# A two-layer GELU block: the first x chunk turned as two 64-row halves, block by block, with layer 1 started on the first blocks

## The chip, the cores and the metric

One core of a Trainium2 chip. The metric is the device time of one execution in microseconds (us), the median of several runs. A difference of less than 2% is called "same"; ratios with a 95% interval resolve some 0.3%. Engines are named as in the profile: PE is TensorE's matmul side, PEld its weight loads, DVE is VectorE, ACT is ScalarE, SP issues DMAs. The span is the time from the first to the last instruction of a traced run; a transfer "lands" when its data has arrived; PSUM is the memory into which TensorE writes here.

## The reference, cut to what matters

```python
B, S, D, F = 1, 2048, 448, 1792            # bf16
def reference(x, w1, b1, w2, b2):
    h = gelu_tanh(einsum("bsd,df->bsf", x, w1) + b1)
    return einsum("bsf,fd->bsd", h, w2) + b2
```

448 is 3 x 128 + 64, so each layer-1 product has three full blocks of 128 input features (k = 0, 1, 2) and a remainder of 64 (k = 3).

## The kernel before: the parts that matter

Layer 1 needs x with features on the partitions. The first chunk of 512 rows is loaded plainly and turned on TensorE; later chunks are turned by DMA. All matmuls of both layers contract 64 rows at a time: part "a" takes one half of the partitions, part "b" the other, for two output tiles at once, so that two matmuls run side by side, one on rows 0 to 63 of the array and one on rows 64 to 127. The 64 remainder rows of w1 are loaded to partitions 64 to 127 only (`w1r`); VectorE copies what the other half needs to partitions 0 to 63.

```python
H = 64; HC = 256; KT = 3; NWARM = 7
W1CUTS = (0, 4, 8, 14)                      # w1 in three transfers, by output tile
unit = [psum_tensor([128, 2, 512], FP32) for i in range(4)]    # two banks each
# ...
def turn(t):                                # 128 rows of x, one full turn for each k
    for k in range(KT):
        tensor.transpose(stage(t)[:, k*P:(k+1)*P], xn[:, t, k*P:(k+1)*P], ident)   # after "x"
def evac(engine, t):                        # PSUM -> xT, 384 columns, for all k; vector and scalar in turn
    ...
def turn_all():
    # vector: xr <- the remainder columns of xn
    # for t in 0..3: turn(t); evac(t)
    # tensor: two turns of xr; then vector and scalar copy them to xT[:, 3] (2 copies each)
# ...
warm(NWARM)          # dummy matmuls of 512 columns until x lands
warm(1, HC)          # half dummy
turn_all()
warm(1, HC)          # half dummy
turn_b1()            # vector: four 32x32 transposes of b1, then a cast
for i in (0, 1):     # vector: w1r, partitions 64..127 -> 0..63, event ("w1rU", i)
    ...
for h in (0, HC):    # pairs 0 and 1 of layer 1, part a, half the columns at a time
    L[0].a(h, h + HC); L[1].a(h, h + HC)
L[0].b(); L[2].a(); L[1].b()
for j in range(3, NPAIR):
    L[j].a(); L[j - 1].b()
L[-1].b()
# ... layer 2 of the chunk; then chunks 1 to 3
```

The matmul of k = 3 in part b waits for `w1r` (one output tile) or for VectorE's copy of it, `w1rU` (the other). VectorE works through its list in the order of the program, so what stands last on that list is done last.

## Time and profile before

| | before |
|---|---|
| median of 6 runs | 94.24 us (93.99 to 94.44) |
| the traced run | 94.75 us, span 93.44 |
| PE busy | 97% of the span |
| first turn / first layer-1 matmul / first w1r matmul | 4.00 / 5.79 / 8.155 us |

The page of the profile, before: busy time by engine (us, share, number of instructions), and the chain of work that ended last.

```profile
span 93.4 us, 2060 instructions
...
PE 90.4 (97%) x932; PEld 46.5 (50%) x932; DVE 13.3 (14%) x33; ACT 38.5 (41%) x63; POOL 1.7 (2%) x8
...
## 4 chain that ended last, share of the span: by engine, by line
PE 97%; DVE 0%; issue 0%
PE u L216 91%; PE u L191 4%; PE u L338 1%; DVE out_sb L325 0%; PE u L359 0%
```

The chain is TensorE's own work from start to end, so the time is TensorE's dense stream plus what comes ahead of it. L216 is the helper that issues every layer-1 and layer-2 matmul.

The timeline of the head, before (start, duration, engine, line, operation, tiles; in brackets the idle time of the engine before it and what ended it):

```profile
4.00 1.44 PE L338 MATMUL u<-ident,xn 128*128 128x128 bf16 x12
...
4.51 0.36 DVE L345 COPY xT<-u 128x384 bf16<-128x384 bf16 x1 [0.40 <-PE u L338]
...
5.44 0.42 PE L191 MATMUL u<-const-bfloat16-1.0 128*128 128x256 bf16 x1
...
5.76 0.60 DVE L368 COPY xT<-u 64x256 bf16<-64x256 bf16 x2 [0.25 <-PE u L359]
...
5.79 2.52 PE L216 MATMUL u<-xT,w_sb 64*128 64x256 bf16 x30
...
6.39 0.90 DVE L180 STREAM_TRANSPOSE b1t<-b1n 32x32 bf16<-32x32 bf16 x4
7.42 0.17 DVE L182 CAST b_f<-b1t 128x14 f32<-128x14 bf16 x1
7.63 0.49 DVE L382 COPY w1r<-w1r 64x256 bf16<-64x256 bf16 x2
...
8.15 0.38 PE L216 MATMUL u<-xT,w1r 64*128 64x512 bf16 x2
```

Read it as two lists. TensorE: turns from 4.00, half dummy at 5.44, layer 1 from 5.79, first w1r matmuls at 8.15. VectorE: a chain with hardly a pause from 5.76 (remainder copies, bias transposes, cast) whose last link, the w1r copy, begins at 7.63; the record of the first of its two parts, the one that pair 0 needs, ends at 7.85. TensorE wanted it for the weight load at 7.94, so VectorE was 0.1 us early.

How fast TensorE runs can be read from counts. Two windows of 0.6 us, before, PE only (us, busy and count, granted clock, DMA share, GB/s):

```profile
core 0: us, PE busy (x), PEclk, DMA share, GB/s
...
5.85:6.45 0.60, 0.60 (x9) 1.00 0.84 260
6.75:7.35 0.60, 0.60 (x16) 1.00 0.95 248
```

Both are fully busy with matmuls of 256 columns, but the second has nearly twice as many: pairs start 214 ns apart up to 6.62 us and 109 ns apart after. The column of the granted clock shows 1.00 in both, so it does not show this.

### The profile page before, as it was taken

The page shows a single profiled execution, that of the slowest core. Times are in us where ns is not written, and L with a number is a line of the kernel's source. Part 1 is how long each engine was busy: PE and PEld are TensorE (multiplying, and loading weights), DVE is VectorE, ACT ScalarE, POOL GpSimd, SP SyncE. Part 2 cuts the span into 40 slices and gives each one's busy share as a digit, 9 for nine tenths or more (in the row PEclk, how much of TensorE's full clock was granted, in tenths as well). Part 3 has the DMA queues.
Part 4 walks back from the last instruction along what each step waited for, and adds up shares of the span by engine and source line. Part 5 has one row for each costly group of instructions (what it writes and reads, how often), then busy time and mean ns, then how long its engine had stood idle before and what let it go on. Part 6 is the DMA issues. An engine that isn't in the chain of part 4 may idle for free.

```text
span 93.4 us, 2060 instructions
## 1 busy us (share of the span) xinstructions
PE 90.4 (97%) x932; PEld 46.5 (50%) x932; DVE 13.3 (14%) x33; ACT 38.5 (41%) x63; POOL 1.7 (2%) x8
## 2 busy tenths in 40 slices
PE   6999999999999999999999999999999999999990
PEld 2475444455544444454554444445544444475890
DVE  0173001010334000000234000000234000000421
ACT  6073787900002887900002888900001878910001
POOL 6000000000000000000000000000000000000000
DMA  2999999554748000000033000000022000000022
GB/s 51 358 275 292 360 309 151 113 113 91 83 86 217 7 0 0 7 0 0 0 102 101 0 0 4 0 7 0 0 98 98 0 0 7 0 0 7 18 80 98
DMA packets 12344, 7.32 MB, mean 78 GB/s; under 512 B 6960, under 2 KB 12144, under 8 KB 12336
## 3 DMA queue, kind: packets, MB, share of 16 engines
q1 hardware_dynamic: 11904, 6.80, 31.1%
q10 hardware_dynamic: 400, 0.39, 1.2%
q8 instruction: 7, 0.11, 0.5%
q14 instruction: 1, 0.01, 0.0%
q0 software_dynamic: 32, 0.00, 0.0%
HBM read 3.79 MB, written 1.84 MB: 60 GB/s over the span
## 4 chain that ended last, share of the span: by engine, by line
PE 97%; DVE 0%; issue 0%
PE u L216 91%; PE u L191 4%; PE u L338 1%; DVE out_sb L325 0%; PE u L359 0%
## 5 line engine op out<-in xcount | busy, mean ns | idle before, releaser
L268 ACT ACTIVATE g<-u,b_f 128x512 bf16<-128x512 f32 x56 | 35.0, 685 | 40.3 <-PE u L216 40.3
L216 PE MATMUL u<-w_sb,g 64*128 64x448 bf16 (+1 forms) x504 | 43.2, 328 | 0.0
L216 PE MATMUL u<-xT,w_sb 64*128 64x512 bf16 (+1 forms) x348 | 41.2, 372 | 0.0
L216 PEld LDWEIGHTS u<-w_sb,g 64*128 64x128 bf16 x504 | 24.4, 94 | 18.6
L216 PEld LDWEIGHTS u<-xT,w_sb 64*128 64x128 bf16 x348 | 16.9, 95 | 19.6 <-issue 0.3
L311 DVE TENSOR_TENSOR out_sb<-u,b_bc 128x448 bf16<-128x448 f32 x14 | 8.1, 619 | 60.6 <-PE u L216 60.6
L216 PE MATMUL u<-xT,w1r 64*128 64x512 bf16 x56 | 10.6, 376 | 0.0
L191 PE MATMUL u<-const-bfloat16-1.0 128*128 128x512 bf16 (+1 forms) x9 | 3.8, 578 | 0.8 <-PEq L443 0.8
L216 PEld LDWEIGHTS u<-xT,w1r 64*128 64x128 bf16 x56 | 2.7, 94 | 3.3
L328 ACT CAST out_sb<-u 128x224 bf16<-128x224 f32 x1 | 0.3, 346 | 9.2 <-PE u L216 9.2
L191 PEld LDWEIGHTS u<-const-bfloat16-1.0 128*128 128x128 bf16 x9 | 1.2, 138 | 2.4 <-issue 2.4
L345 ACT COPY xT<-u 128x384 bf16<-128x384 bf16 x2 | 1.0, 479 | 2.8 <-PE u L338 2.8
L175 ACT ACT_TABLE_LOAD x1 | 1.3, 1283 | 0.7 <-PEq L443 0.7
L338 PEld LDWEIGHTS u<-ident,xn 128*128 128x128 bf16 x12 | 1.2, 140 | 0.5 <-issue 0.5
L338 PE MATMUL u<-ident,xn 128*128 128x128 bf16 x12 | 1.4, 307 | 0.0
L186 DVE COPY xT<-xT 64x512 bf16<-64x512 bf16 x3 | 0.9, 290 | 3.5 <-DMA xT<-in_x_dram 3.5
L406 DVE COPY b_z<-b_bc 1x448 bf16<-1x448 bf16 x1 | 0.3, 267 | 6.8 <-DMA b_bc<-in_b_dram 6.8
L319 DVE TENSOR_TENSOR out_sb<-u,b_bc 128x448 bf16<-128x448 f32 x1 | 0.6, 625 | 1.7 <-PE u L216 1.7
L180 DVE STREAM_TRANSPOSE b1t<-b1n 32x32 bf16<-32x32 bf16 x4 | 0.8, 202 | 0.1
L345 DVE COPY xT<-u 128x384 bf16<-128x384 bf16 x2 | 0.7, 357 | 0.7 <-PE u L338 0.7
L368 ACT COPY xT<-u 64x256 bf16<-64x256 bf16 x2 | 0.7, 368 | 0.0
L352 DVE COPY xr<-xn 128x256 bf16<-128x256 bf16 x1 | 0.2, 227 | 3.0 <-DMA xn<-in_x_dram 3.0
(18 smaller groups left out, 5.0 us busy)
## 6 DMA issues: line engine op xcount, KB each, us to landing
out_dram<-out_sb SPq DMA_DIRECT2D x16, 112.0 KB, 1.7
w_sb<-in_w_dram SPq DMA_DIRECT2D x2, 784.0 KB, 8.7
w_sb<-in_w_dram SPq DMA_DIRECT2D x1, 576.0 KB, 6.4
xn<-in_x_dram SPq DMA_DIRECT2D x1, 448.0 KB, 3.1
w_sb<-in_w_dram ACTq DMA_DIRECT2D x1, 384.0 KB, 4.2
w_sb<-in_w_dram SPq DMA_DIRECT2D x1, 384.0 KB, 4.1
xT<-in_x_dram SPq DMA_TRANSPOSE x12, 4.5
w1r<-in_w_dram SPq DMA_DIRECT2D x1, 160.0 KB, 4.0
```

What stands on the lines that cost most here:

```text
L175: pr.op("scalar", lambda e: e.activation(junk[:, :], one, ACT.Gelu_apprx_tanh), event="table")
L180: pr.op("vector", lambda e, q=q: e.transpose(b1t[32 * q:32 * q + 32, :], b1n[:, 32 * q:32 * q + 32]), after=["b1n"], event=("b1t", q))
L186: pr.op("vector", lambda e: e.tensor_copy(xT[0:H, KT, s0:s1], xT[H:P, KT, s0:s1]), after=after, event=event)
L191: pr.op("tensor", lambda e: e.matmul(unit[0][:, 0, 0:cols], lhsT=ones_w, rhs=ones_m[:, 0:cols], start=True, stop=True))
L216: o = pr.op("tensor", lambda e: e.matmul(unit[u][:, lo, cols], lhsT=lhsT, rhs=rhs, start=start, stop=stop, skip_group_check=skip), after=a ...
L268: pr.op("scalar", lambda e, lo=lo, ft=ft: e.activation(g[:, ft, c * SC:(c + 1) * SC], unit[u][:, lo, :], ACT.Gelu_apprx_tanh, bias=b1_f[:, ...
L311: pr.op("vector", lambda e, lo=lo, j=j: e.tensor_tensor(out=out_sb[:, j, :], in0=unit[u][:, lo, 0:D], in1=b2_bc[:, :], op=ALU.add), after= ...
L319: pr.op("vector", lambda e: e.tensor_tensor(out=out_sb[:, j, :].rearrange("p (two h) -> p two h", two=2), in0=unit[u][:, :, 0:DH], in1=b2_ ...
L328: pr.op("scalar", lambda e: e.copy(out_sb[:, j, DH:D], unit[u][:, 1, 0:DH]), after=[y[1]], event=("o", j, 1))
L338: pr.op("tensor", lambda e, k=k: e.transpose(stage(t)[:, k * P:(k + 1) * P], xn[:, t, k * P:(k + 1) * P], ident[:, :]), after=["ident", "x ...
L345: pr.op(engine, lambda e: e.copy(o, i) if engine == "scalar" else e.tensor_copy(o, i), after=[("xt", t)], event=("xT0", t))
L368: e.copy(o, i) if engine == "scalar" else e.tensor_copy(o, i),
```

## The change

The intent: turn x in pieces of 64 rows, two side by side on the two halves of the array, so that a turn streams 64 columns instead of 128; drain each 128 x 256 block as soon as it is turned; let layer 1 wait for the block it reads, not for whole tiles; fill TensorE's wait by starting pair 0 and put the last turns inside it; load w1's first tiles as 2 + 2 so that the first lands earlier; drop the half dummies, and with them the switch from 128-row to 64-row matmuls after the turns.

```diff
-        W1CUTS = (0, 4, 8, 14)
+        W1CUTS = (0, 2, 4, 8, 14)
...
         load_w1(0, "scalar")
+        load_w1(1, "scalar")
...
-                            after += ([("xT0", 2 * h), ("xT0", 2 * h + 1)] if k < KT else
+                            after += ([("xT0", h, k)] if k < KT else
...                                             (turn, evac, turn_all replaced by:)
+        def turn(o, i, event, after):           # two turns of 64 rows, on the two halves of the array
+            for half, rows in enumerate(HALVES):
+                pr.op("tensor", lambda e, half=half, rows=rows: e.transpose(o(half), i(rows), ident[rows, rows]), ...)
+        def turn_block(h, k, u, i, wait=()):    # 256 rows of x, block k: two such turns
+        def drain_blocks(engine, h, ks, u, wait=None):     # PSUM -> xT, 256 columns for each block
+        def turn_first():
...                                             (vector: xr copy)
+            for k, engine in enumerate(("vector", "scalar", "vector")):
+                turn_block(0, k, k, 0)
+                drain_blocks(engine, 0, (k,), k)
+            turn_block(1, 0, 3, 0)
+            turn_block(1, 1, 3, 1)
+            drain_blocks("scalar", 1, (0, 1), 3)
+        def turn_rest():
+            turn_block(1, 2, 2, 0, [("xT0", 0, 2)])
...                                             (two remainder turns of xr into the same banks)
+            drain_blocks("vector", 1, (2,), 2, ("xr", 1))
...                                             (remainder copies, as before, after that drain)
         warm(NWARM)
-        warm(1, HC)
-        turn_all()
-        warm(1, HC)
+        turn_first()
+        L = [Layer1(0, j) for j in range(NPAIR)]
+        L[0].a(0, HC)
+        turn_rest()
         turn_b1()
...                                             (w1r copies, unchanged)
-        for h in (0, HC):
-            L[0].a(h, h + HC)
-            L[1].a(h, h + HC)
+        L[1].a(0, HC)
+        L[0].a(HC, SC)
+        L[1].a(HC, SC)
         L[0].b()
+        L[1].b()
         L[2].a()
-        L[1].b()
```

More of the change, by code (lines that the diff above doesn't have):

```diff
@@ L155, in bass_standalone__dense_activation_gelu__prompt_kernel @@
         load_w1r(0)
-        load_w1(1)
+        load_w1(2)
         load_w1r(1)
-        load_w1(2)
+        load_w1(3)
         load_w2(0, 7)
@@ L330, in drain, with spot @@
                     store(j, [("o", j, 0), ("o", j, 1)])
-        def stage(t):
-            return unit[3 - t // 2][:, t % 2, 0:2 * P].bitcast(BF16)
-        def turn(t):
-            for k in range(KT):
-                pr.op("tensor", lambda e, k=k: e.transpose(
-                    stage(t)[:, k * P:(k + 1) * P], xn[:, t, k * P:(k + 1) * P], ident[:, :]),
-                    after=["ident", "x"], event=("xt", t) if k == KT - 1 else None)
-        def evac(engine, t):
-            o = xT[:, 0:KT, t * P:(t + 1) * P]
-            i = stage(t)[:, 0:D3].rearrange("p (k s) -> p k s", k=KT)
-            pr.op(engine, lambda e: e.copy(o, i) if engine == "scalar" else e.tensor_copy(o, i),
-                  after=[("xt", t)], event=("xT0", t))
-            busy[(3 - t // 2, t % 2)] = ("xT0", t)
-        def turn_all():
+        HALVES = (slice(0, H), slice(H, P))
+        def spot(u, i, rows=slice(0, P)):
+            return unit[u][rows, :, i * H:(i + 1) * H].bitcast(BF16).rearrange("p b (t s) -> p b t s", t=2)
+        def turn(o, i, event, after):
+            for half, rows in enumerate(HALVES):
+                pr.op("tensor", lambda e, half=half, rows=rows: e.transpose(o(half), i(rows), ident[rows, rows]),
+                      after=["ident"] + after, event=event if half else None)
+        def turn_block(h, k, u, i, wait=()):
+            for t in (0, 1):
+                turn(lambda half, t=t: spot(u, i)[:, half, t, :], lambda rows, t=t: xn[rows, 2 * h + t, k * P:(k + 1) * P],
+                     ("xt", h, k) if t else None, ["x"] + list(wait))
+        def drain_blocks(engine, h, ks, u, wait=None):
+            n = len(ks)
+            o = xT[:, ks[0]:ks[0] + n, h * HC:(h + 1) * HC].rearrange("p k (t b s) -> p k b t s", b=2, t=2)
+            f = unit[u][:, :, 0:n * H].bitcast(BF16).rearrange("p b (k t s) -> p k b t s", k=n, t=2)
+            for i in range(n):
+                pr.op(engine, lambda e, i=i: (e.copy if engine == "scalar" else e.tensor_copy)(o[:, i], f[:, i]),
+                      after=[wait or ("xt", h, ks[-1])], event=("xT0", h, ks[i]))
+            busy[(u, 0)] = ("xT0", h, ks[-1])
+        def turn_first():
             pr.op("vector", lambda e: e.tensor_copy(
@@ L354, in turn_all @@
                 xn[:, :, D3:D].rearrange("p (q two) h -> p q two h", two=2)), after=["x"], event="xr_in")
-            for t in range(STC):
-                turn(t)
-                evac(("vector", "scalar")[t % 2], t)
+            for k, engine in enumerate(("vector", "scalar", "vector")):
[6 more added lines that the diff above has]
+            turn_block(1, 2, 2, 0, [("xT0", 0, 2)])
             for q in range(STC // 2):
-                pr.op("tensor", lambda e, q=q: e.transpose(
-                    stage(0)[:, q * P:(q + 1) * P], xr[:, q, :], ident[:, :]),
-                    after=["xr_in", ("xT0", 0)], event=("xr", q))
-            halves = (slice(0, H), slice(H, P))
+                turn(lambda half, q=q: spot(2, 1)[:, half, q, :], lambda rows, q=q: xr[rows, q, :], ("xr", q), ["xr_in"])
+            drain_blocks("vector", 1, (2,), 2, ("xr", 1))
             for src, engine in enumerate(("vector", "scalar")):
-                i = stage(0)[halves[src], 0:2 * P].rearrange("p (q s) -> p q s", q=2)
+                i = spot(2, 1, HALVES[src])
                 for dst in (src, 1 - src):
-                    o = xT[halves[dst], KT, 0:SC].rearrange("p (q two s) -> p q two s", q=2, two=2)[:, :, src, :]
+                    o = xT[HALVES[dst], KT, 0:SC].rearrange("p (q two b s) -> p b q two s", q=2, two=2, b=2)[:, :, :, src, :]
                     pr.op(engine, lambda e, o=o, i=i, engine=engine:
                           e.copy(o, i) if engine == "scalar" else e.tensor_copy(o, i),
-                          after=[("xr", 0), ("xr", 1)], event=("xR0", dst, src))
-            busy[(3, 0)] = ("xR0", 1, 0)
-            busy[(3, 2)] = ("xR0", 0, 1)
+                          after=[("xr", 1), ("xT0", 1, 2)], event=("xR0", dst, src))
+            busy[(2, 1)] = ("xR0", 1, 0)
+            busy[(2, 2)] = ("xR0", 0, 1)
         warm(NWARM)
-        warm(1, HC)
-        turn_all()
-        warm(1, HC)
+        turn_first()
+        L = [Layer1(0, j) for j in range(NPAIR)]
+        L[0].a(0, HC)
+        turn_rest()
         turn_b1()
@@ L383, in bass_standalone__dense_activation_gelu__prompt_kernel @@
                   after=[("w1r", i)], event=("w1rU", i))
-        L = [Layer1(0, j) for j in range(NPAIR)]
-        for h in (0, HC):
-            L[0].a(h, h + HC)
-            L[1].a(h, h + HC)
+        L[1].a(0, HC)
+        L[0].a(HC, SC)
+        L[1].a(HC, SC)
         L[0].b()
+        L[1].b()
         L[2].a()
-        L[1].b()
         for j in range(3, NPAIR):
```

## The prediction

> **What bounds the kernel.** TensorE. The chain of waits puts 97% of the span on it; the timeline shows it dense from 5.8 us (first layer-1 matmul) to 91.3 us. So the change can only move the moment at which the dense stream reaches a given point. My mark: the start of the first w1r (64-row remainder) matmul, part b of pair 0, 8.155 us in the trace.
>
> **The head now (timeline by engine).** x lands at 3.86 us, the first turn starts at 4.00. The 14 turns are spaced 107 ns and the layer-1 pairs of 256 columns 214 ns, up to about 6.65 us; then the same pairs 109 ns. That is the half-rate clock of the Trainium skill's "TensorE: Matmul & The Clock Gate" (Part 1: half rate until a sustained busy window has passed); the trace agrees. Turns end 5.44, half dummy to 5.65, then 0.14 us idle before the first 64-row matmul (the skill's "TensorEngine Tiling (Array Packing)", Key Properties: a change of tiling mode drains the array). VectorE runs without a pause from 5.76: remainder copies (2 x 0.31), four bias transposes (4 x 0.23), bias cast, then the copy of w1r to the other rows, ending at 7.85. The mark needs that copy, with only 0.1 to 0.3 us of slack.
>
> **What the change does.**
> - Removes: two half dummies (0.21 us each; only the second is on the path), the mode switch after the turns, half the streaming of each turn. A pair of 64-row turns should start every 55 ns (half of 107; estimate), 110 ns if weight loads bind.
> - Splits w1's first 384 KB: its first half should land near 4.5 us instead of 4.99 (estimate from packet times).
> - Moves: drains become 256 columns (VectorE 0.285, ScalarE 0.37 us, from the remainder copies). First drain about 4.35 to 4.63; first layer-1 matmul about 4.73 instead of 5.79. Pairs 214 ns apart to 5.37, then the last turns to 5.6.
> - By 6.65 TensorE is some 0.4 us ahead, and would reach the mark near 7.75.
>
> **Why that gain is not kept.** The last turns now come after pair 0's first half. VectorE's drain of the last block waits for the second remainder turn, so it starts at about 5.83; then a wait on its own result (0.13 us, as before the bias cast), then the same 2.09 us chain (remainder copies, bias, w1r copy) that took 5.76 to 7.85. w1r is ready at 5.83 + 0.42 + 2.09 = about 8.35, and the mark is reached at about 8.45 instead of 8.155: TensorE stalls about 0.6 us in pair 0's part b, and the program ends 0.3 us later. With 110 ns turn pairs it is +0.8 us. Everything after the mark (L1.b before L2.a) should be neutral.
>
> **Predicted: 94.5 us**, 8 in 10 within 93.95 to 95.2. Chances: faster by over 2%: 0.01; within 2%: 0.97; slower by over 2%: 0.02.
>
> **What would show it.** First layer-1 matmul near 4.7; turn pairs 55 ns apart; TensorE idle for 0.4 to 0.8 us just before a w1r matmul near 8.4, released by VectorE's w1r copy; VectorE idle from about 4.95 to 5.8; full rate still from near 6.65; after the mark the same stream, shifted as the mark is.
>
> **What would make it wrong.** The clock: 0.3 us more idleness between 3.7 and 4.8 could delay full rate by a window (+1.3 us), or bring it earlier (no gain, VectorE's chain binds). Slower drains of 64-element runs. x or w1 landing later, which shifts the chain one for one. If VectorE's chain is shorter than 2.5 us, a gain of up to 0.4 us appears: about 93.8.

## The result, and the profile after

| | before | after |
|---|---|---|
| median of 6 runs | 94.24 us | 94.64 us (94.60 to 94.85) |
| ratio | | 1.0047 (1.0030 to 1.0064) |
| traced run: time, span | 94.75, 93.44 | 94.85, 93.51 |
| first layer-1 matmul | 5.79 | 4.79 |
| w1r copy done | 7.85 | 8.28 |
| w1r matmuls of pair 0 | 8.155 and 8.157 | 7.667 and 8.338 |

A ratio is the mean time of one kernel's runs over that of the other's of the same rounds, so it is not quite the ratio of the medians. Executions over 1.5% slower than the fastest of the same kernel are left out of the means. By the 2% rule the two are the same; the interval says that the change made the kernel some 0.4 us slower.

The page after:

```profile
span 93.5 us, 2084 instructions
...
PE 90.1 (96%) x944; PEld 50.4 (54%) x944; DVE 13.5 (14%) x34; ACT 38.5 (41%) x64; POOL 1.7 (2%) x8
...
## 4 chain that ended last, share of the span: by engine, by line
PE 94%; DVE 2%; issue 1%; ACT 0%; DVEq 0%
PE u L217 90%; PE u L192 3%; PE u L344 1%; DVE b1t L181 1%; DVE xT L384 1%; ACT out_sb L329 0%; DVE xT L357 0%; DVE w1r L399 0%; DVE b_f L183 0%; DVEq L63 0%
```

The chain now has VectorE's work of the head in it (before, it had VectorE only in the last drain). The same chain in order of time, after (start, duration, what):

```profile
4.79 0.82 PE u L217 x6
5.61 0.23 PE u L344 x8
...
5.86 0.30 DVE xT L357
...
6.19 0.28 DVE xT L384
...
8.06 0.23 DVE w1r L399
...
8.34 82.99 PE u L217 x868
```

From 5.86 to 8.29 the program hangs on VectorE alone (left out between the shown pieces: the second remainder copy, four bias transposes and the cast). The timeline of the head, after:

```profile
4.02 0.72 PE L344 MATMUL u<-ident,xn 64*128 64x64 bf16 x20
...
4.35 0.51 DVE L357 COPY xT<-u 128x256 bf16<-128x256 bf16 x2 [0.21 <-PE u L344]
...
4.79 0.82 PE L217 MATMUL u<-xT,w_sb 64*128 64x256 bf16 x6
...
5.38 0.34 PE L344 MATMUL u<-ident,xn 64*128 64x64 bf16 x4
...
5.50 0.32 PE L344 MATMUL u<-ident,xr 64*128 64x64 bf16 x4
...
5.61 2.22 PE L217 MATMUL u<-xT,w_sb 64*128 64x256 bf16 x24
5.86 0.29 DVE L357 COPY xT<-u 128x256 bf16<-128x256 bf16 x1 [1.01 <-PE u L344]
6.19 0.60 DVE L384 COPY xT<-u 64x256 bf16<-64x256 bf16 x2
...
6.82 0.90 DVE L181 STREAM_TRANSPOSE b1t<-b1n 32x32 bf16<-32x32 bf16 x4
...
7.67 0.38 PE L217 MATMUL u<-xT,w1r 64*128 64x512 bf16 x1
7.85 0.18 DVE L183 CAST b_f<-b1t 128x14 f32<-128x14 bf16 x1
8.06 0.22 DVE L399 COPY w1r<-w1r 64x256 bf16<-64x256 bf16 x1
...
8.34 0.39 PE L217 MATMUL u<-xT,w1r 64*128 64x512 bf16 x1 [0.29 <-DVE w1r L399]
```

The lines answer those of before one by one. The first 20 of the 28 turns of 64 rows take 4.02 to 4.74 (eight come later); before, all 14 full turns took 4.00 to 5.44. The first drain is at 4.35, layer 1 starts at 4.79: one us earlier. But VectorE idles 1.01 us ahead of the drain at 5.86, because that block is turned only behind pair 0's first half, and its chain ends at 8.28 instead of 7.85. Of the two w1r matmuls one uses the loaded rows and goes at 7.67; the other needs the copied rows and goes at 8.34. Before, they went together.

The clock in this trace was much as in the first trace of before: by the starts of the matmuls, pairs of 256 columns are 213 ns apart up to 6.44 us and 109 ns after, the turns of 64 columns 53 ns from pair to pair.

### The profile page after: what moved, and what is told of

Read it like the earlier page. It is cut to its first block, busy times and chain, and to the rows that moved or that the text cites. A ratio compares the mean times of both kernels' runs of the same rounds, so it can differ in the third digit from the quotient of the medians.

```text
span 93.5 us, 2084 instructions
## 1 busy us (share of the span) xinstructions
PE 90.1 (96%) x944; PEld 50.4 (54%) x944; DVE 13.5 (14%) x34; ACT 38.5 (41%) x64; POOL 1.7 (2%) x8
## 3 DMA queue, kind: packets, MB, share of 16 engines
HBM read 3.79 MB, written 1.84 MB: 60 GB/s over the span
## 4 chain that ended last, share of the span: by engine, by line
PE 94%; DVE 2%; issue 1%; ACT 0%; DVEq 0%
PE u L217 90%; PE u L192 3%; PE u L344 1%; DVE b1t L181 1%; DVE xT L384 1%; ACT out_sb L329 0%; DVE xT L357 0%; DVE w1r L399 0%; DVE b_f L183 0%; DVEq L63 0%
## 5 line engine op out<-in xcount | busy, mean ns | idle before, releaser
L217 PE MATMUL u<-xT,w_sb 64*128 64x512 bf16 (+1 forms) x348 | 43.8, 374 | 0.1
L217 PEld LDWEIGHTS u<-w_sb,g 64*128 64x128 bf16 x504 | 28.7, 94 | 14.1
L217 PEld LDWEIGHTS u<-xT,w_sb 64*128 64x128 bf16 x348 | 19.8, 96 | 19.2 <-issue 0.2
L217 PE MATMUL u<-xT,w1r 64*128 64x512 bf16 x56 | 16.7, 376 | 0.3 <-DVE w1r L399 0.3
L217 PEld LDWEIGHTS u<-xT,w1r 64*128 64x128 bf16 x56 | 5.3, 94 | 4.1 <-DVE w1r L399 0.8
L192 PE MATMUL u<-const-bfloat16-1.0 128*128 128x512 bf16 x7 | 3.1, 624 | 0.8 <-PEq L459 0.8
L357 ACT COPY xT<-u 128x256 bf16<-128x256 bf16 x3 | 1.0, 374 | 2.2 <-PE u L344 2.2
L344 PEld LDWEIGHTS u<-ident,xn 64*128 64x128 bf16 x24 | 0.9, 127 | 1.0 <-issue 1.0
L344 PE MATMUL u<-ident,xn 64*128 64x64 bf16 x24 | 1.1, 238 | 0.1
L357 DVE COPY xT<-u 128x256 bf16<-128x256 bf16 x3 | 0.8, 292 | 1.2 <-PE u L344 1.2
```

Of the source, the lines that this page charges most:

```text
L192: pr.op("tensor", lambda e: e.matmul(unit[0][:, 0, 0:cols], lhsT=ones_w, rhs=ones_m[:, 0:cols], start=True, stop=True))
L217: o = pr.op("tensor", lambda e: e.matmul(unit[u][:, lo, cols], lhsT=lhsT, rhs=rhs, start=start, stop=stop, skip_group_check=skip), after=a ...
L344: pr.op("tensor", lambda e, half=half, rows=rows: e.transpose(o(half), i(rows), ident[rows, rows]), after=["ident"] + after, event=event i ...
L357: pr.op(engine, lambda e, i=i: (e.copy if engine == "scalar" else e.tensor_copy)(o[:, i], f[:, i]), after=[wait or ("xt", h, ks[-1])], eve ...
```

## The experiments

Each was timed in five rounds against the kernel before on the same chip, on four chips; the median of before was 94.20 to 94.40 us, so medians can be compared to some 0.2 us. "After" below is the changed kernel. x lands at another time in each run (3.74 to 4.24 us), so where traces are compared I count from the landing of x, as the trace records it.

| run | median us | ratio to before | full rate from, us | x lands | w1r copy done, after x | 2nd w1r matmul, after x | span less x |
|---|---|---|---|---|---|---|---|
| before | 94.24 | 1 | 6.6 | 3.86 | 3.99 | 4.30 | 89.58 |
| before again | 94.25 | 0.9999 | before 4.1 | 3.89 | 3.48 | 3.54 | 88.87 |
| after | 94.64 | 1.0047 | 6.4 | 3.88 | 4.40 | 4.46 | 89.63 |
| after again | 94.68 | 1.0056 | before 4.35 | 4.17 | 3.95 | 4.01 | 89.18 |
| chain longer | 95.37 | 1.0105 | before 4.3 | 4.07 | 4.68 | 4.73 | 89.90 |
| w1r copy early | 94.01 | 0.9966 | 6.0 | 4.07 | 1.96 | 3.49 | 88.78 |
| turns first only | 94.36 | 1.0013 | before 4.35 | 4.15 | 3.62 | 3.67 | 88.83 |

"Full rate from" is the moment from which successive pairs start half as far apart as at first.

### Control: the kernel before again

No edit.

> The kernel before, unchanged, as a control. Ratio 1.00 under every theory. The trace of before that I read was of a run at 94.75 us, 0.5 us above its median. Clock theory: the moment at which layer-1 pairs of 256 columns go from 214 to 109 ns apart differs between runs (6.65 us in the first trace); a faster run of before shows it earlier, by two times the time gained. If the moment is again 6.65 within 0.1, the clock doesn't explain the spread of before.

Measured: 94.25 us, ratio 0.9999 (0.9954 to 1.0045). This trace is of a run at 94.08 us. The window of 5.85 to 6.45 us, which held 9 matmuls of 256 columns in the first trace, holds 16 here:

```profile
5.85:6.45 0.60, 0.60 (x16) 1.00 0.78 278
```

Already the 128-column turns at 4.02 us are 55 ns apart instead of 107. So the moment of full rate differs from run to run, by 2.5 us or more, and the first trace of before was of a late one. I had expected the moment to move by twice the time gained, 1.3 us for the 0.67 us between the two traced runs; it moved further. Part of what TensorE gained it waited away: its weight load for the remainder turns waited 0.18 us for a drain, and the second w1r matmul came 0.25 us after the first. The spans of before's 11 runs of this call lie between 92.7 and 93.6 us. One more thing shows in this trace: with full rate from the start, before meets VectorE's chain as well.

```profile
5.21 2.13 PE L216 MATMUL u<-xT,w_sb 64*128 64x256 bf16 x30
...
7.15 0.22 DVE L382 COPY w1r<-w1r 64x256 bf16<-64x256 bf16 x1
7.18 0.64 PE L216 MATMUL u<-xT,w1r 64*128 64x512 bf16 x2
7.42 0.09 PEld L216 LDWEIGHTS u<-xT,w1r 64*128 64x128 bf16 x1 [0.37 <-DVE w1r L382]
```

The copy starts at 7.15, and the weight load at 7.42 waited for it. Of the two traces of before, only the one with a late clock has the slack that I had read.

### The w1r copy early

```diff
         L[0].a(0, HC)
+        copy_w1r(0)        # taken from behind turn_b1(), where copy_w1r(1) stays
         turn_rest()
```

> The kernel after, with VectorE's copy of the first w1r part taken out of the end of its chain and put ahead of the drain of the last block, where VectorE was idle from 4.85 to 5.86 us. Chain theory: the pause of 0.67 us before the second w1r matmul (7.667 to 8.338) vanishes and the program is 0.55 to 0.67 us faster than after: about 94.05, ratio to before 0.998. Rival, the pause costs nothing because the loss is of the clock or of the start-up (dummies gone): no pause, but the time stays at 94.6, ratio 1.004.

Measured: 94.01 us, ratio 0.9966 (0.9929 to 1.0003), against 1.0047 for after: 0.63 us faster by the medians, and no stall. The timeline of its head:

```profile
5.81 0.22 DVE L392 COPY w1r<-w1r 64x256 bf16<-64x256 bf16 x1 [0.77 <-DMA w1r<-in_w_dram]
6.05 0.29 DVE L357 COPY xT<-u 128x256 bf16<-128x256 bf16 x1
...
7.54 0.39 PE L217 MATMUL u<-xT,w1r 64*128 64x512 bf16 x2
```

The copy sits where VectorE idled (the w1r rows it copies landed at 5.79), and the two w1r matmuls go together again at 7.54. The chain theory holds; the rival, that the loss lay elsewhere, would have left 94.6.

### The chain made longer

```diff
         turn_b1()
+        for q in range(4):
+            pr.op("vector", ... e.transpose(b1j[32*q:32*q+32, :], b1n[:, 32*q:32*q+32]) ...)   # result unused
```

> The kernel after, with four more bias transposes (0.93 us, result unused) in VectorE's chain ahead of the w1r copy. Chain theory: the second w1r matmul moves from 8.34 to 9.27 us and the time grows by 0.93: about 95.55, ratio 1.014. Rival (the pause is absorbed later): under 0.3 us more.

Measured: 95.37 us, ratio 1.0105 (1.0067 to 1.0142). The four extra transposes, whose result nobody waits for, started 0.21 us apart and not 0.23, the first of them 0.08 us after the start of the cast, so they added 0.73 us (start of the cast to start of the copy: 0.94 us, against 0.21 in after). My figure of 0.93 was wrong. The median grew by 0.73, the ratio by less (0.0058, some 0.55 us, with an interval of 0.35 us to either side). The traces are sharper: against after again, also with an early clock, the copy is done 0.73 us later after x and the span less x is 0.72 us longer, so the delay passes one to one. The wait of the weight load, by the view of waits (us in total, times, longest):

```profile
PEld u L218 <- DVE w1r L403: 1.7, 1, 1.7
```

### w1's first four tiles in one transfer

```diff
-        W1CUTS = (0, 2, 4, 8, 14)
+        W1CUTS = (0, 4, 8, 14)       # and the loads as before
```

> The kernel after, with w1's first four tiles in one transfer again, as before. Chain theory: this transfer lands at 5.0 instead of 4.5 us, the first layer-1 matmul starts at 5.05 instead of 4.79, the last turns, the drain and the whole VectorE chain come 0.25 us later: about 94.9, ratio 1.007. Rival (768 descriptors of 512 B hold up the later transfers, w1's tiles 4 to 8 landed at 8.2 instead of 7.0 us in after): landings as in before and a time of 94.6 or less.

Measured: 94.82 us, ratio 1.0041 (1.0002 to 1.0080); one of its six runs was slow (96.22) and is left out of the ratio. The transfer landed at 4.95 and the first layer-1 matmul started at 4.99, as expected, though x had landed at 3.74, the earliest of all traces. Tiles 4 to 7 landed at 6.79 instead of 8.2, as the rival said. In time the run decides nothing: 1.0041 is within the noise of both. Counted from x its trace, which has an early clock, bears the chain theory out: against after again the copy is done 0.40 us later (4.35 instead of 3.95) and the span less x is 0.40 us longer (89.58 instead of 89.18). That x landed 0.43 us earlier hid it in the time.

### The w1r copy early, in the kernel before

```diff
+        copy_w1r(0)
         turn_b1()
         copy_w1r(1)
```

> The kernel before, with the first w1r copy put ahead of the bias transposes on VectorE. Chain theory: before has slack in late-clock runs (mark 8.155, copy done 7.85) and a stall of about 0.2 us only in early-clock runs (control trace: copy done 7.371, second w1r matmul 7.427), so it gains 0 to 0.2 us: about 94.1, ratio 0.997 to 1.0. If it gains as much as the same move gave after (0.6 us: 93.6), the chain bound both kernels alike and the prediction's reason for the difference is wrong. What this kernel and the after kernel with the early copy (94.01) differ by is what the rest of the change is worth.

Measured: 94.44 us, ratio 1.0021 (0.9991 to 1.0051). The same move that gave after 0.6 us gives before nothing that could be resolved; it was not in the range that I had set, but within its noise. So the chain did not bind both kernels alike: the change made it the bound, where before meets it only with an early clock, and then by 0.25 us.

### The old order of pairs 1 and 2

```diff
         L[0].b()
-        L[1].b()
         L[2].a()
+        L[1].b()
```

> The kernel after, with pair 2's part a ahead of pair 1's part b again, as before. My theory: neutral, 94.65 within 0.15, since the order only says what fills the array beside and after the late w1r matmul. Rival: the w1 tile of pairs 2 and 3 landed at 7.8 to 8.2 us in after and its kin (7.0 in before), so pair 2's part a first would wait for it: up to 0.2 us slower where the mark is earlier than the landing; in after the mark is at 8.34, so no wait is expected.

Measured: 94.54 us, ratio 1.0025 (0.9996 to 1.0054): neutral. The tile that pair 2 needs landed at 7.58, a full microsecond ahead of the second w1r matmul at 8.60, so there was no wait for it. This trace has a late clock (6.5 us) and a span less x of 89.62, the same as after's 89.63.

### The half dummy back

```diff
         warm(NWARM)
+        warm(1, HC)        # on the kernel with the early w1r copy
```

> After with the early w1r copy and the half dummy ahead of the turns back. My theory: nothing on the path (it ends at 3.94, x lands at 3.86 to 4.07): 94.0 within 0.15. Rival (the missing dummy delays the moment of full clock): 0.2 us or more faster, and less spread.

Measured: 94.04 us, ratio 0.9982 (0.9953 to 1.0012), against 94.01 without it: neutral. The traced run had full rate only from 6.5 us, so the dummy does not bring it forward either, as far as one trace shows.

### Control: after again

No edit.

> The kernel after, unchanged, as a control, to see what the clock does to it. Ratio to before 1.004 within 0.003 if the first comparison holds. In traces with a late full clock (6.5 us or later) the two kernels' spans, counted from the landing of x, differ by 0.05 us only (89.63 and 89.58). Theory: before is bound by TensorE in its head and gains 0.7 us from an early clock (88.87), after is bound by VectorE's chain and gains less (0.45 by the run with the longer chain, less the 0.73 that was added). So if this trace shows an early clock, span less x is about 89.2; if a late one, 89.6. If it is 88.9 in an early one, the interplay with the clock is not the reason.

Measured: 94.68 us, ratio 1.0056 (1.0025 to 1.0086). The trace has an early clock (64-column turns in pairs 28 ns apart from the start, 53 in the first trace) and a span less x of 89.18, as the theory said. Its head:

```profile
5.70 0.29 DVE L357 COPY xT<-u 128x256 bf16<-128x256 bf16 x1 [0.63 <-PE u L344]
...
7.21 0.38 PE L217 MATMUL u<-xT,w1r 64*128 64x512 bf16 x1
...
7.89 0.22 DVE L399 COPY w1r<-w1r 64x256 bf16<-64x256 bf16 x1
...
8.17 0.39 PE L217 MATMUL u<-xT,w1r 64*128 64x512 bf16 x1 [0.59 <-DVE w1r L399]
```

The first w1r matmul goes at 7.21, but the second still waits for the copy that starts at 7.89. Counted from x, TensorE came to the first of them 0.74 us sooner than in the first trace (3.04 instead of 3.79), the copy was done only 0.45 us sooner, and TensorE's idle time before the second is 0.59 us instead of 0.29. With a late clock the change costs 89.63 - 89.58 = 0.05 us, with an early one 89.18 - 88.87 = 0.31 us, each figure from one trace of each kernel.

### The last turns with the first ones, nothing else

```diff
             turn_block(1, 0, 3, 0)
             turn_block(1, 1, 3, 1)
-            drain_blocks("scalar", 1, (0, 1), 3)
+            turn_block(1, 2, 3, 2)
+            ...                                   # both remainder turns, into the same two banks
+            drain_blocks("vector", 1, (0, 1, 2), 3, ("xr", 1))
...                                             (and out of turn_rest, but for the remainder copies)
```

> The kernel after with the last turns done with the first ones, and the w1r copy left at the end of VectorE's chain. This undoes only 'last turns inside layer 1'. Chain theory: the drain of the last block starts 1.43 us after x instead of 1.98, the w1r copy and the stall's end come 0.55 earlier, 3.85 instead of 4.40 us after x, and the time is 94.1, ratio 0.9985. Rival (the place of the last turns doesn't matter): ratio 1.004.

Measured: 94.36 us, ratio 1.0013 (0.9984 to 1.0042). The direction is right and the size too large: compared with after at an early clock, the w1r copy is done 3.62 instead of 3.95 us after x and the span less x falls by 0.34 us. I had taken the 1.98 us of a late-clock trace for the start of the last drain; at an early clock it was 1.53 after x in after, and 1.21 here. A stall of 0.68 us between the w1r matmuls remains, since the bias work still stands before the copy. The edit undoes a little more than its text says: the drains of blocks 0 and 1 of the second half, which ScalarE did, are now VectorE's, so this run does not show the place of the turns quite alone.

### Both: turns first and the w1r copy early

> After with the early w1r copy, and the last turns put with the others (all 14 pairs at once, in the same two banks) instead of inside pair 0. Theory: TensorE does them in the 0.25 us in which it waits for the first drain anyway, so first layer-1 matmul unchanged (about 0.9 us after the first turn... 0.75 at the late clock), no turns between layer-1 matmuls, w1r matmul some 0.2 us earlier, time 0.1 to 0.2 below the 94.01 of the early copy alone: about 93.85, ratio 0.996. Rival: the drains of the second half, all on VectorE now and waiting for the last turn, come later and make TensorE wait in pair 0's second half: no gain or a loss of up to 0.3.

Measured: 93.92 us, ratio 0.9959 (0.9931 to 0.9986). The timeline:

```profile
4.08 0.76 PE L344 MATMUL u<-ident,xn 64*128 64x64 bf16 x24 [0.16 <-DMA xn<-in_x_dram]
...
4.85 2.37 PE L217 MATMUL u<-xT,w_sb 64*128 64x256 bf16 x30
5.41 1.31 PEld L217 LDWEIGHTS u<-xT,w_sb 64*128 64x128 bf16 x24 [0.34 <-DMA w_sb<-in_w_dram]
...
7.06 0.38 PE L217 MATMUL u<-xT,w1r 64*128 64x512 bf16 x2
...
10.55 0.11 PEld L217 LDWEIGHTS u<-xT,w_sb 64*128 64x128 bf16 x4 [0.51 <-DMA w_sb<-in_w_dram]
```

All turns fit into 4.08 to 4.91 (the last remainder turn is not shown), layer 1 starts at 4.85 and the w1r matmuls go together at 7.06. The rival's stall for the drains did not come. What TensorE now waits for is w1: weight loads idle 0.34 us at 5.41 until tiles 2 and 3 land (5.37), 0.40 us at 8.20 until tiles 4 to 7 land (8.16), and 0.51 us at 10.55 until tiles 8 to 13 land.

### w1's tiles 8 and 9 apart

```diff
-        W1CUTS = (0, 2, 4, 8, 14)
+        W1CUTS = (0, 2, 4, 8, 10, 14)        # on the kernel just above
```

> All turns first and the early w1r copy (93.92 before), with w1's tiles 8 and 9 in a transfer of their own. In the trace of that kernel TensorE waited 0.18 us at 10.16 us for the transfer of w1's tiles 8 to 13, landed at 10.51. Theory: this wait goes, 93.75, ratio 0.994. Rival: the transfers are bound by rate and more packets make the others later (tiles 4 to 7 at 8.16 already cost 0.06): no gain.

Measured: 93.74 us, ratio 0.9955 (0.9929 to 0.9981). The wait at 10.2 us is gone from the trace; the wait for tiles 2 and 3 ahead of pair 1 is still there (its first matmul at 5.72, tiles landed at 5.67). The median is lower by what was expected, the ratio by less than its noise.

### The same with w1's first four tiles in one transfer

> The fastest kernel so far (turns first, early w1r copy, w1's tiles 8 and 9 apart; 93.74, ratio 0.9955) with w1's first four tiles in one transfer again. In the nine traces with the 2+2 split x landed at 4.07 us in the mean (3.88 to 4.24), in the four without it at 3.89 (3.74 to 4.06). If the split itself delays x by holding its last packets up, x lands at about 3.9 here, w1 at 4.95, the first layer-1 matmul starts near 5.0 against 4.95 in the mean with the split, and the time is the same within 0.1: ratio 0.995 to 0.997. If x's landing only scatters, the first matmul could have started at 4.75 with the split and starts at 5.0 without it: 0.25 us slower, ratio 0.998.

Measured: 93.78 us, ratio 0.9946 (0.9911 to 0.9980), so the same as with the split. But its trace does not settle why: x landed at 3.95 us and w1 at 5.27, so that the first layer-1 matmul waited until 5.32. Five traces without the split now have x at 3.90 us in the mean (3.74 to 4.06), nine with it at 4.07 (3.88 to 4.24); the ranges overlap. The landings of w1 show why the split is worth little here: in the nine traces with it tiles 0 and 1 land at 4.71 us in the mean and tiles 2 and 3 at 5.45, in the five without it all four at 5.06. Pair 0 can start earlier and pair 1 later, and with no turns between them TensorE waits for tiles 2 and 3; in this trace it starts late, but then shows no such wait.

The last two kernels beat both, by about 0.5 us against before and 0.9 us against after. Both are below the 2% that counts as a difference.

## Why the prediction was right, point by point

- **The time.** 94.5 was predicted, 94.64 measured, 0.40 us above before by the medians where I had said about 0.3. The range held it.
- **The gain in TensorE's head.** Turn pairs at 55 ns: 53 measured. First layer-1 matmul near 4.73: 4.79. TensorE ready for the w1r matmul near 7.75: 7.67. All right, in a trace whose clock was as late as that of the trace I had read.
- **Why it is not kept.** VectorE idle from 4.95 to 5.8: 4.85 to 5.86. The w1r copy done at 8.35: 8.28. The mark at 8.45: 8.34 for the second w1r matmul; the first, which is the mark as I had worded it, went at 7.67. Stall of 0.4 to 0.8 us: 0.67 between the starts of the two; the profile counts 0.29 of it as idle. The longer chain (0.73 us added, 0.72 measured from x) and the early copy (-0.63) show that this is the cause, and the same move in before (no gain) shows that it is so only after the change. Turning the last blocks first took 0.34 us back from x on, 0.32 by the medians, so it is mainly the part "last turns inside layer 1" that delayed the chain (with the reservation made at that run).
- **A term that was mis-sized.** "The program ends 0.3 us later", with "after the mark the same stream, shifted as the mark is". In the two first traces the mark moved by 0.18 us and the end by only 0.07. Only one of the two w1r matmuls waits: the other ran 0.67 us ahead, and the late one was paired with the next pair's first matmul (8.338 and 8.342). One half of the array so kept a lead of one matmul. The other traces agree that this is worth 0.12 us: from the second w1r matmul to the end of the span it is 85.16 to 85.17 us in all six with such a stall, and 85.28 to 85.33 in seven of the eight others (85.56 in "turns first and the copy early", which then waits for w1). How the lead saves the time was not tested.
- **A step that was wrong.** "Full rate still from near 6.65." I had one trace and took its clock as given. It was a late one; in the control full rate came before 4.1 us. With an early clock the change costs 0.31 us, with a late one 0.05. So the medians agree with my figure partly by luck: too much for the clock that I had assumed, about right for an early one. My caveat for an earlier clock, "no gain, VectorE's chain binds", had the right engine but not the size: after gained 0.45 us from it, from x on, and before 0.71.
- **What stays open.** The medians differ by 0.40 and 0.48 us and the ratios by 0.0047 and 0.0056, more than the 0.05 to 0.31 that the traces show from the landing of x on. The later landing of x in the traces with the split w1 (0.17 us in the mean) would fill most of it, but it may be scatter: the two runs without the split were no faster, and in both of their traces the first layer-1 matmul came right after w1's landing (4.99 after 4.95, 5.32 after 5.27), so they don't tell.

## What to carry to other kernels

When the bounding engine is fed sooner, ask which other engine's list now ends last: here TensorE came half a microsecond sooner to the mark, and a copy that had no hurry before became the end of VectorE's chain because one link of it, the drain of the last block, was moved behind other work. Put what others wait for ahead of what nobody waits for yet, in the engine's idle time. And take a control trace of the kernel before: in which state its clock was decides what slack a timeline shows.

## What the Trainium skill lacked or had wrong

- "TensorE: Matmul & The Clock Gate", Part 4, says that full clock does not engage for transposes. Here, behind seven or eight dummy matmuls, the turns did run at full rate: 128-column turns started 55 ns apart in the control of before, against 107 ns in the first trace, and pairs of 64-column turns 28 ns apart in the control of after, against 53. Whether turns alone would bring the full rate no run shows.
- The same page, Part 1, has the moment of full clock depend on the phase of a free-running window. The runs show how far it moves for one kernel: before 4.1 us in one trace of before and 6.6 us in another, 0.7 us of the span, and more than the 500 ns to either side that the page gives. That the window is the reason no run shows. The page calls the ramp negligible for modelling (under 1% of a span); 0.7 of 93.4 us is under 1%, but here it is larger than the effect of the change, 0.4 us.
- No page gives a case in which the granted clock of a profile reads 1.00 in a stretch at half rate: 9 and 16 matmuls of the same width in 0.6 us, both under 1.00.
- "TensorEngine Tiling (Array Packing)", Key Properties, says that a change of tiling mode drains the array but not what this costs: from the end of the half dummy's streaming (5.444 us plus half of 427 ns) to the first 64-row matmul TensorE idled 0.14 us at the half rate, and 0.10 us (5.001 plus 0.107 to 5.205) at the full rate in the control of before; in both the data for that matmul was there. That the drain is the reason is the page's word, no run tests it.
- No page says what it does to the pairing when one of two row-tiled matmuls meant to run side by side waits: the first went 0.67 us ahead, the late one ran beside the next instruction (8.338 and 8.342 us), and the stream from there to the end was 0.12 us shorter than in the traces without such a wait.
